# Seven products instead of eight in three groups of part 0, and attention issued in whole tiles

## The chip, the core and the metric

The kernel runs on one core of a Trainium2 chip. The metric is the time of one execution on the device in microseconds (us). The core has a matrix engine (TensorE; its products are called PE and its weight loads PEld below), VectorE (DVE), ScalarE (ACT), GpSimd (POOL) and a sequencer that issues the transfers (SP). They run side by side and wait for one another by semaphores. Products land in PSUM, which has 8 banks; DVE and ACT read them there, POOL cannot.

## The reference

Causal attention with a window of 128 positions and a slope per head, then two MLPs, all on 2304 tokens of 512 features, in float32:

```python
# attention: 4 sequences of 576 tokens, 8 heads of 64
scores = scale * q @ k.T
mask = (rel >= 0) & (rel < 128)            # rel = own position - other position
attn = softmax(where(mask, scores + bias, -1e9))
x = (attn @ v) as [2304, 512]
# first MLP, d_ff = 1536
g = x @ w_gate
x = (g * sigmoid(g) * (x @ w_val)) @ w_out
# second MLP, d_ff = 2048
h = x @ w_in
out = (h * sigmoid(h)) @ w_out2
```

The inputs arrive as 64-bit numbers.

## The kernel before

**Parts and groups.** The 18 tiles of 128 tokens are cut into three parts of 6 tiles, and a part into two halves of 384 tokens (N = 384). Each part goes through attention, the first MLP in G1 = 6 groups of 256 hidden features (`moe1`, for part 0 `moe1_plain`), and the second in G2 = 8 groups (`moe2`). The attention of part 1 runs between the MLP products of part 0, that of part 2 between those of part 1.

**Precision.** Each operand is held as a high and a low piece, and each product is three passes (hi·hi, hi·lo, lo·hi), lines 762 to 764, 906 to 908 and 936 to 938. So every value that becomes an operand is copied (mostly ACT, line 301) and the copy subtracted from it (POOL line 311 or DVE line 310).

**Plain groups and quads.** A plain group computes [256 features] x [512 inputs] x [two token halves] as eight block products, a quad as seven by Strassen's scheme (`quad`). A quad needs seven weight blocks: the three given ones A11, A12, A22 and four sums S1 to S4. It also needs seven activation blocks: `operands` makes them from the stored activations into the seven slots of `XOP` (slots 0, 1, 2 hold given blocks, 3 to 6 sums and differences). Part 0 uses plain groups in the first MLP: its attention writes the four given blocks straight into `XOP`, in slots 0, 1, 2 and 6.

**Weights.** `raw_weight` loads 64-bit weights and turns them into 32-bit words (ACT line 660, DVE line 663). In mode "raw" `quad_weights` makes the sums, splits all seven blocks and stores them to DRAM. In mode "kept" it loads the seven blocks. In mode "sum" (part 1, first MLP) it loads the stored words and three blocks, and makes and stores the four sums. All transfers are issued by SP from one queue in a written order.

**Order.** Every operation is entered into a `Plan` with its engine, a cost, a due time, what it reads and writes and the PSUM banks that it takes. `issue` then walks through a model of the engines and writes the instructions of each engine out in one fixed order. For a bank it keeps limits by kind: "mm" for MLP products, "S" for scores, "att" for all attention, and so on. So a change of costs, due times or dependencies moves instructions on every engine.

**Attention per half tile.** For each tile and each half of the heads: `prepare` turns k and q (PE lines 398 and 406, identity products), `score` makes 12 products on 64 rows of the array (line 448) into two banks, DVE masks and reduces, ACT takes exponents, POOL normalizes (line 497), PE turns the result (line 515), POOL cuts it into two triangles (lines 522 and 529), and `weigh` multiplies with v on 64 columns (line 541). The MLP products use the whole 128x128 array. `out1` and `out2` are the second products of the MLPs (lines 906 and 936); they lie in `pend` until `flush` enters them after the next group's first products, and DVE adds their results into `ACC` (lines 920 and 948).

Of the kernel before, what the change touches and what calls it, by code (L numbers as in the profile page):

```python
# [9 lines left out]
F32 = mybir.dt.float32  # L10
# [10 lines left out]
P = 128  # L21
# [180 lines left out]
def attention_moe_moe2_kernel(  # L202
# [32 lines left out]

    nc = tc.nc
# [9 lines left out]
    G1, G2 = F1 // (2 * P), F2 // (2 * P)  # L246
    NU, NO, NRAW, NW, NH, NTMP = 17, 3, 2, 3, 6, 8
# [33 lines left out]
    U_R = ring(2, [P, 4, P], F32, "u")  # L281
    L_R = ring(1, [P, 4, P], F32, "l")
# [11 lines left out]
    plan = Plan(BANKS, {"mm": 6, "att": 4, "T": 1, "S": 3, "C": 2, "O": 1, "B": 4})  # L294
# [129 lines left out]
    def attend(i, hf, dues):  # L424
        n = 2 * i + hf
        qt, qk = QT_R[n % len(QT_R)], ("qt", n % len(QT_R))
# [5 lines left out]
        heads = slice(4 * hf, 4 * hf + 4)  # L432

        banks = [Bank("S"), Bank("S")]

        def score():
            for p in range(2):
                for x, y in ((0, 0), (0, 1), (1, 0)):  # L440
                    for e in range(2):
                        rows = slice(64 * e, 64 * e + 64)
                        view = banks[e].tile.rearrange("p (a b c) -> p a b c", a=2, b=2)
                        rhs = KR[rows, y, 2 * hf + p]
                        dst = view[:, p]
                        if first(i):
                            rhs, dst = rhs[:, s], dst[:, 0]
                        nc.tensor.matmul(  # L448
                            dst, qt[rows, x, p, :], rhs, start=(x == 0 and y == 0), stop=(x == 1)
                        )  # L450

        reads = [qk, ("KR", s, hf)] + ([] if first(i) else [("KR", 1 - s, hf)])
        plan.add("pe", 6 * 118 + 60, dues[0], score, reads, banks, take=tuple(banks))
# [55 lines left out]
        cb, ob = Bank("C"), Bank("O")  # L509
        cps = lambda: cb.tile.rearrange("p (a b) -> p a b", b=P)  # L510
        ops = lambda: ob.tile[:, 0:2 * P].rearrange("p (a b) -> p a b", b=P)
# [22 lines left out]
        parts = [(i, u)] if first(i) else [(i - 1, u), (i, lo)]  # L534

        def weigh():
            for p in range(2):
                for a, (tl, m) in enumerate(parts):
                    for j in range(2):
                        l = 2 * p + j  # L540
                        nc.tensor.matmul(  # L541
                            ops()[64 * j:64 * j + 64, p, :],
                            VLD_R[tl % len(VLD_R)][:, 4 * hf + l, :],
                            m[:, l, :],
                            start=(a == 0),
                            stop=(a == len(parts) - 1),
                        )

        reads = [uk] + ([] if first(i) else [lk]) + [x for tl, _ in parts for x in loaded(tl, "v", hf)]
        plan.add("pe", 540 * len(parts) + 60, due, weigh, reads, [ob], take=ob)  # L550
        ti = i % PT
        xt = XST[:, ti, 2 * hf:2 * hf + 2, :]
        xk = [("xt", ti, 2 * hf + p) for p in range(2)]
        if i >= PT:
            copy_op(256, due, lambda: xt, ops, [ob], xk, give=ob)
        else:
# [3 lines left out]
            copy_op(256, due, lambda: xh, ops, [ob], keys)  # L560
            plan.add(
                "dve", cost("dve", 256), due,
                lambda: nc.vector.tensor_tensor(xl, ops(), xh.bitcast(F32), ALU.subtract), [ob], keys, give=ob,  # L563
# [16 lines left out]
    def split(dst_slot, kk, src, reads, due, bank=None):  # L580
# [4 lines left out]
        copy_op(N, due, lambda: hi_ap, src, reads, keys, psum=psum)  # L585
        sum_op(N, due, lambda: lo_ap, src, lambda: hi_ap.bitcast(F32), ALU.subtract, reads, keys, give=bank, psum=psum)

    def operands(src, name, due):

        due -= 25000.0  # L590

# [509 lines left out]
```

## Time and profile before

| | |
|---|---|
| median of 3 runs | 954.29 us (953.21 to 955.04) |
| the profiled execution | 954.24 us, of which the span from first to last instruction is 952.5 us |
| PE busy in the span | 931.7 us (98%) |
| DVE, ACT, POOL busy | 644.8, 499.2, 352.9 us (68%, 52%, 37%) |
| 16 DMA engines | 68.2% of their time, 219 GB/s of HBM traffic |
| mean granted TensorE clock | 0.998 of full speed |

Busy time of PE counts a product from its start to its modelled end, and products overlap in the array; so a stretch in which PE is busy throughout can still hold time that a different order of products would save. The distance from one product's start to the next one's start tells that. Parts 0, 1 and 2 of the MLPs take about 27 to 376, 376 to 660 and 660 to 952 us of the span.

### The profile page before, as it was taken

What the parts mean: (1) busy time and instruction counts of PE and PEld (TensorE: products, weight loads), DVE (VectorE), ACT (ScalarE), POOL (GpSimd) and SP (SyncE); (2) the same over time, 40 slices, a digit from 0 to 9 for tenths busy, and PEclk for the clock granted to TensorE, in tenths of its full rate; (3) what the DMA queues carried; (4) which work ended last, traced back from release to release, by engine and by line L of the source; (5) the groups of instructions that cost most, each with busy time, mean ns of one, the idle gap of its engine ahead of it and who ended that gap; (6) DMA issues with size and microseconds to landing.
All of it is one profiled execution on the core that took longest, in us unless ns stands there. A gap on an engine that the chain in (4) does not pass through costs nothing.

```text
span 952.5 us, 16827 instructions
## 1 busy us (share of the span) xinstructions
PE 931.7 (98%) x5662; PEld 854.8 (90%) x5662; DVE 644.8 (68%) x1489; ACT 499.2 (52%) x1269; POOL 352.9 (37%) x426
## 2 busy tenths in 40 slices
PE   7999999998999999999999999999999999999998
PEld 5888989998887888999999998888899999988886
DVE  7886666758798889557666756657745555855655
ACT  6877555556866765665453564345343323553331
POOL 2645333347666788796651521111200000300000
PEclk9999999999999999999999999999999999999999
DMA  9978897776578987998766666355466666654522
GB/s 216 276 240 253 271 301 260 256 241 207 189 255 262 293 266 259 362 285 287 227 200 185 198 201 191 125 167 184 162 239 201 208 214 215 204 198 170 161 89 89
DMA packets 156854, 209.78 MB, mean 220 GB/s; under 512 B 65760, under 2 KB 86496, under 8 KB 156768
## 3 DMA queue, kind: packets, MB, share of 16 engines
q1 hardware_dynamic: 156768, 208.71, 68.2%
q8 instruction: 45, 0.74, 0.3%
q14 instruction: 41, 0.34, 0.1%
HBM read 146.28 MB, written 62.39 MB: 219 GB/s over the span
## 4 chain that ended last, share of the span: by engine, by line
PE 86%; DVE 7%; DMA 3%; ACT 2%; POOL 1%; issue 1%; SPq 0%; DVEq 0%; ACTq 0%; POOLq 0%
PE bank L762 15%; PE bank L763 14%; PE bank L764 14%; PE bank L936 6%; PE bank L938 6%; PE bank L937 6%; PE bank L906 5%; PE bank L907 5%; PE bank L908 5%; PE bank L448 3%; PE bank L541 3%; DVE word L663 2%; PE bank L515 1%; DMA raw<-in_moe_w_in_dram 1%; DVE bank L464 1%
## 5 line engine op out<-in xcount | busy, mean ns | idle before, releaser
L762 PE MATMUL bank<-XOP,wu 128*128 128x384 f32 (+2 forms) x880 | 301.5, 343 | 6.7 <-DVE qt L412 2.1
L763 PE MATMUL bank<-XOP,wu 128*128 128x384 f32 (+2 forms) x880 | 293.8, 334 | 0.6 <-DVE XOP L563 0.5
L764 PE MATMUL bank<-XOP,wu 128*128 128x384 f32 (+2 forms) x880 | 294.0, 334 | 0.1
L762 PEld LDWEIGHTS bank<-XOP,wu 128*128 128x128 f32 x880 | 165.5, 188 | 15.9 <-ACT tmp L301 2.8
L763 PEld LDWEIGHTS bank<-XOP,wu 128*128 128x128 f32 x880 | 165.8, 188 | 2.2 <-DVE XOP L563 0.7
L764 PEld LDWEIGHTS bank<-XOP,wu 128*128 128x128 f32 x880 | 165.6, 188 | 0.4 <-POOL wu L311 0.4
L311 POOL TENSOR_TENSOR h<-tmp,h 128x384 fp32r<-128x384 f32 x67 | 71.3, 1074 | 194.7 <-ACT h L301 186.4
L301 ACT ACTIVATE tmp<-bank 128x384 f32<-128x384 f32 x140 | 65.5, 489 | 108.1 <-PE bank L764 73.3
L936 PE MATMUL bank<-wo,h 128*128 128x512 f32 x290 | 116.1, 400 | 0.5 <-DVE ACC L948 0.5
L938 PE MATMUL bank<-wo,h 128*128 128x512 f32 x290 | 114.0, 393 | 0.0
L937 PE MATMUL bank<-wo,h 128*128 128x512 f32 x290 | 113.9, 393 | 0.0
L948 DVE TENSOR_TENSOR ACC<-bank,ACC 128x512 f32<-128x512 f32 (+1 forms) x127 | 86.0, 682 | 32.5 <-PE bank L938 32.0
L865 DVE SCALAR_TENSOR_TENSOR tmp<-tmp,bank 128x384 f32<-128x384 f32 (+2 forms) x128 | 68.6, 544 | 53.4 <-ACT tmp L855 43.7
L906 PE MATMUL bank<-h,wo 128*128 128x384 f32 (+2 forms) x296 | 100.9, 341 | 0.0
L907 PE MATMUL bank<-h,wo 128*128 128x384 f32 (+2 forms) x296 | 98.5, 333 | 0.6 <-POOL h L311 0.6
L908 PE MATMUL bank<-h,wo 128*128 128x384 f32 (+2 forms) x296 | 98.6, 333 | 0.0
L802 DVE TENSOR_TENSOR bank<-bank,tmp 128x384 f32<-128x384 f32 x96 | 53.8, 561 | 52.9 <-PE bank L764 41.1
L301 ACT ACTIVATE h<-tmp 128x384 fp32r<-128x384 f32 x102 | 52.5, 521 | 61.3 <-PE bank L937 35.2
L920 DVE TENSOR_TENSOR ACC<-bank,ACC 128x384 f32<-128x384 f32 x120 | 65.3, 553 | 22.8 <-PE bank L908 22.5
L855 ACT ACTIVATE tmp<-bank 128x384 f32<-128x384 f32 (+2 forms) x134 | 63.2, 482 | 32.7 <-PE bank L764 19.4
L311 POOL TENSOR_TENSOR wu<-word,wu 128x256 fp32r<-128x256 f32 x69 | 52.3, 775 | 61.9 <-ACT wu L301 47.4
L497 POOL TENSOR_TENSOR c<-c,st 128x512 f32<-128x512 f32 x36 | 39.1, 1087 | 93.6 <-DVE st L494 91.1
(98 smaller groups left out, 1580.5 us busy)
## 6 DMA issues: line engine op xcount, KB each, us to landing
wo<-kept_o SPq DMA_DIRECT2D x56, 512.0 KB, 4.1
wu<-kept_i SPq DMA_DIRECT2D x112, 256.0 KB, 3.6
wu<-kept_g SPq DMA_DIRECT2D x60, 256.0 KB, 3.6
wu<-kept_v SPq DMA_DIRECT2D x60, 256.0 KB, 3.9
raw<-in_moe_w_out_dram SPq DMA_DIRECT2D x28, 512.0 KB, 4.6
kept_o<-wo SPq DMA_DIRECT2D x28, 512.0 KB, 3.8
kept_i<-wu SPq DMA_DIRECT2D x56, 256.0 KB, 2.9
kept_g<-wu SPq DMA_DIRECT2D x42, 256.0 KB, 4.3
```

The source lines that it names most:

```text
L301: act = lambda: nc.scalar.activation(out(), src(), AF.Copy)
L311: pool = lambda: nc.gpsimd.tensor_tensor(out(), x(), y(), op)
L762: nc.tensor.matmul(ps, wh, xh, start=start, stop=False, skip_group_check=True)
L763: nc.tensor.matmul(ps, wh, xl, start=False, stop=False, skip_group_check=True)
L764: nc.tensor.matmul(ps, wl, xh, start=False, stop=stop, skip_group_check=True)
L906: nc.tensor.matmul(ps[:, 0:n], wh, h[:, 0], start=(i == 0), stop=False)
L907: nc.tensor.matmul(ps[:, 0:n], wh, h[:, 1], start=False, stop=False)
L908: nc.tensor.matmul(ps[:, 0:n], wl, h[:, 0], start=False, stop=(i == 1))
L936: nc.tensor.matmul(ps, hh, wh, start=(i == 0), stop=False)
L937: nc.tensor.matmul(ps, hh, wl, start=False, stop=False)
L938: nc.tensor.matmul(ps, hl, wh, start=False, stop=(i == 1))
L948: plan.add("dve", cost("dve", n), due, lambda: nc.vector.tensor_tensor(acc, pv(), acc, ALU.add), [b], keys, give=b)
```

## The change

1. Part 0's first MLP uses plain groups only for groups 0 to 2 (GP = 3). `restore` puts part 0's attention output, high plus low piece, into `XST`; `operands` with `plain=False` makes the four slots 3 to 6 that are sums; and groups 3 to 5 run as quads in mode "raw". Part 1 then takes groups 3 to 5 in mode "kept".
2. From tile 6 on (EARLY = 6) the scores of both halves of a tile are one plan entry that takes four banks, and so are the two weighings, into one bank. The buffers `u` and `l` get one more each, the "S" limit goes from 3 to 4, "att" from 4 to 6. A copy of 512 columns takes the weighed tile to `XST`, instead of two of 256.
3. The out-products of the second token half are entered before those of the first, in `moe1` and `moe2`.
4. Part 1's attention gets due times 33 us apart, three tiles before the border between the two MLPs and three from 20 us behind it. Before, the six tiles were spread evenly.

```diff
+    EARLY = 6
+    GP = 3
...
-    U_R = ring(2, [P, 4, P], F32, "u")
-    L_R = ring(1, [P, 4, P], F32, "l")
+    U_R = ring(3, [P, 4, P], F32, "u")
+    L_R = ring(2, [P, 4, P], F32, "l")
...
-    plan = Plan(BANKS, {"mm": 6, "att": 4, "T": 1, "S": 3, "C": 2, "O": 1, "B": 4})
+    plan = Plan(BANKS, {"mm": 6, "att": 6, "T": 1, "S": 4, "C": 2, "O": 1, "B": 4})
...
+    def score(i, halves, due):
...
+        take = tuple(b for hf in halves for b in banks[hf])
+        plan.add("pe", 6 * 118 * len(halves) + 290, due, products, reads, list(take), take=take)
+        return banks
...
-        plan.add("pe", 6 * 118 + 60, dues[0], score, reads, banks, take=tuple(banks))
...
-        plan.add("pe", 540 * len(parts) + 60, due, weigh, reads, [ob], take=ob)
+        plan.add("pe", 218 * len(halves) * (1 if first(i) else 2) + 290, due, product, reads, [ob], take=ob)
...
+    def restore(due):
...
+        for j in range(2):
+            for blk in range(2):
+                for kk in range(2):
+                    c, slot = 2 * j + kk, x_slot(j, blk)
+                    hi, lo = (tiles(XOP[:, slot, i, kk].bitcast(F32)) for i in range(2))
+                    dst = XST[:, blk * BT:blk * BT + BT, c, :]
+                    sum_op(
+                        N, due, lambda dst=dst: dst, lambda hi=hi: hi, lambda lo=lo: lo, ALU.add,
+                        x_keys(slot, kk), [("xt", blk * BT + t, c) for t in range(BT)],
+                    )
...
-            for hf in range(2):
-                prepare(i, hf, at(i + 0.5 * hf) - 8000.0)
-                attend(i, hf, [at(i + p / NP) for p in (2 * hf, 2 * hf + 1)])
+            for halves in [(0,), (1,)] if i < EARLY else [(0, 1)]:
+                t0 = at(i + 0.5 * halves[0])
+                for hf in halves:
+                    prepare(i, hf, t0 - 8000.0)
+                banks = score(i, halves, t0)
+                for hf in halves:
+                    attend(i, hf, [at(i + p / NP) for p in (2 * hf, 2 * hf + 1)], banks[hf])
+                weigh(i, halves, at(i + 0.5 * halves[-1] + 1 / NP))
...
-            for b in range(2):
+            for b in (1, 0):
...
-            for t in range(PT):
+            for t in (*range(BT, PT), *range(BT)):
...
     attention_part(0, ramp)
     moe1_plain([0])
-    spread(1, state["t"] + 6000.0, M1 * (G1 - 1) / G1 + M2 - 8000.0)
-    moe1_plain(range(1, G1))
+    t_next = state["t"] + 6000.0
+    moe1_plain(range(1, GP))
+    restore(state["t"] - 10000.0)
+    operands(XST, "xt", state["t"], plain=False)
...
+    t_moe2 = t_next - 6000.0 + (G1 - GP) * 22 * pe_cost(6, N) + (GP - 1) * 24 * pe_cost(6, N)
+    early = lambda x: t_next + 0.0 + (x - PT) * 33000.0
+    attention_part(1, lambda x: early(x) if x < PT + PT // 2 else t_moe2 + 20000.0 + (x - PT - PT // 2) * 33000.0)
+    moe1(0, range(GP, G1), "raw", False)
     flush()
     operands(ACC, "acc", state["t"])
...
-    moe1(1, range(G1), "sum", False)
+    moe1(1, range(GP), "sum", False)
+    moe1(1, range(GP, G1), "kept", False)
```

Three places show what the plan makes of it. The first is PE at the end of part 1's second MLP, where the last attention tile of part 2 is weighed between out-products (`wo` and `h` are the out-product's operands, `u`, `l` and `vld` the weighing's). Before, the second half of the tile, with the first half 120 rows earlier:

```order
L938 MATMUL bank_138<-wo_92,h_103 128x512
L541 MATMUL bank_139<-u_131,vld_122 64x128 x2
L541 MATMUL bank_139<-l_132,vld_123 64x128 x2
L541 MATMUL bank_139<-u_131,vld_122 64x128 x2
L541 MATMUL bank_139<-l_132,vld_123 64x128 x2
L936 MATMUL bank_133<-wo_91,h_108 128x512
```

and in the changed kernel:

```order
L982 MATMUL bank_139<-wo_92,h_104 128x512
L563 MATMUL bank_138<-u_131,vld_122 64x128 x2
L563 MATMUL bank_138<-l_133,vld_123 64x128 x2
L563 MATMUL bank_138<-u_131,vld_122 64x128 x2
L563 MATMUL bank_138<-l_133,vld_123 64x128 x2
L563 MATMUL bank_138<-u_132,vld_122 64x128 x2
L563 MATMUL bank_138<-l_134,vld_123 64x128 x2
L563 MATMUL bank_138<-u_132,vld_122 64x128 x2
L563 MATMUL bank_138<-l_134,vld_123 64x128 x2
L980 MATMUL bank_142<-wo_91,h_107 128x512
```

Both halves now stand in one run of PE, in one bank; the score products are joined in the same way. Counted over all of PE's rows, runs of score products that follow a product of the full array (an MLP product or a turn) go from 34 to 22, runs of weighings from 34 to 20, and PE has 36 rows fewer, all of them of lines 762 to 764.

The second place is POOL while part 0's first MLP is in its later groups (`word` is a converted weight, `wu` a split block, `sum` one of S1 to S4). Before, in a stretch of the plain groups:

```order
L311 TENSOR_TENSOR wu_74<-word_97,wu_74 128x256
L522 AFFINE_SELECT l_132<-u_130 128x512
L529 AFFINE_SELECT u_130<-u_130 128x512
L311 TENSOR_TENSOR wo_91<-word_98,wo_91 128x512
L311 TENSOR_TENSOR wu_76<-word_98,wu_76 128x256
L311 TENSOR_TENSOR wu_75<-word_98,wu_75 128x256
L311 TENSOR_TENSOR wu_77<-word_96,wu_77 128x256
```

and in the changed kernel, for one quad of group 3:

```order
L314 TENSOR_TENSOR sum_99<-word_96 128x256
L314 TENSOR_TENSOR sum_100<-sum_99,word_98 128x256
L314 TENSOR_TENSOR sum_101<-word_98,word_96 128x256
L314 TENSOR_TENSOR sum_102<-word_98,sum_100 128x256
L314 TENSOR_TENSOR wu_88<-sum_100,wu_88 128x256
L314 TENSOR_TENSOR wu_89<-sum_99,wu_89 128x256
L314 TENSOR_TENSOR wu_73<-word_98,wu_73 128x256
L314 TENSOR_TENSOR wu_76<-word_96,wu_76 128x256
```

The four sums and their splits, which stood in part 1, now stand here. Between the first of the 24 sums of groups 3 to 5 and the first sum of the second MLP, POOL has 88 operations: 40 splits of weight blocks, 24 sums, 9 splits of hidden values, 10 selections, 4 normalizations and 1 split of an out-weight.

The third place is DVE at the border between part 0's two MLPs, where `operands` turns `ACC` into the slots of `XOP`. Before (`st`, `KR` and `qt` belong to attention, `word` to a weight):

```order
L605 TENSOR_TENSOR bank_137<-ACC 128x384
L605 TENSOR_TENSOR bank_136<-ACC,bank_137 128x384
L310 TENSOR_TENSOR XOP<-bank_140,XOP 128x384
L401 TENSOR_TENSOR KR<-bank_133,KR 128x2x128
L310 TENSOR_TENSOR XOP<-bank_136,XOP 128x384
L310 TENSOR_TENSOR XOP<-bank_137,XOP 128x384
L493 TENSOR_SCALAR st_128<-st_128 128x4
L494 RECIPROCAL st_128<-st_128 128x4
L663 SCALAR_TENSOR_TENSOR word_96<-raw_93,top_95 128x512
L605 TENSOR_TENSOR bank_137<-ACC 128x384
L802 TENSOR_TENSOR bank_135<-bank_135,tmp_111 128x384
L412 SCALAR_TENSOR_TENSOR qt_125<-bank_133,qt_125 128x256
```

and in the changed kernel:

```order
L415 SCALAR_TENSOR_TENSOR qt_124<-bank_137,qt_124 128x256
L649 TENSOR_TENSOR bank_140<-ACC 128x384
L649 TENSOR_TENSOR bank_139<-ACC,bank_140 128x384
L404 TENSOR_TENSOR KR<-bank_135,KR 128x2x128
L649 TENSOR_TENSOR bank_138<-ACC 128x384
L313 TENSOR_TENSOR XOP<-bank_139,XOP 128x384
L649 TENSOR_TENSOR bank_137<-ACC,bank_138 128x384
L313 TENSOR_TENSOR XOP<-bank_140,XOP 128x384
L415 SCALAR_TENSOR_TENSOR qt_125<-bank_141,qt_125 128x256
L313 TENSOR_TENSOR XOP<-bank_137,XOP 128x384
L313 TENSOR_TENSOR XOP<-bank_138,XOP 128x384
```

The preparation of an attention tile (`KR`, `qt`) still stands among the operands; the softmax (`st`) and the weight conversion (`word`) no longer do.

## Rows read from the trace of the kernel before

**Rows 1.** The page, part 1: busy us, share of the span, instructions.

```profile
PE 931.7 (98%) x5662; PEld 854.8 (90%) x5662; DVE 644.8 (68%) x1489; ACT 499.2 (52%) x1269; POOL 352.9 (37%) x426
```

**Rows 2.** Windows: length, busy PE, PEld, DVE, ACT, POOL, clock, DMA share, GB/s.

```profile
0.00:27.00 27.00, 20.45 (x151) 14.99 (x151) 21.30 (x102) 18.50 (x67) 7.77 (x15) 1.00 0.89 215
...
146.00:229.00 83.00, 83.00 (x539) 80.01 (x538) 56.37 (x133) 47.17 (x118) 39.31 (x50) 1.00 0.76 248
...
229.00:241.00 12.00, 9.44 (x47) 7.72 (x47) 11.40 (x24) 8.74 (x20) 6.17 (x5) 0.88 0.62 182
241.00:376.00 135.00, 131.15 (x740) 112.56 (x739) 111.96 (x213) 94.34 (x234) 102.27 (x118) 1.00 0.79 258
376.00:830.00 454.00, 452.66 (x2702) 425.70 (x2701) 285.90 (x641) 208.24 (x518) 143.09 (x172) 1.00 0.65 213
```

**Rows 3.** Timeline of PE, twelve full-array products of 384 columns: start, length.

```profile
303.94 0.33 PE L762 MATMUL bank<-XOP,wu 128*128 128x384 f32 x1
...
305.85 0.34 PE L764 MATMUL bank<-XOP,wu 128*128 128x384 f32 x1
```

**Rows 4.** Timeline of products and weight loads around one run of scores.

```profile
316.06 0.40 PE L938 MATMUL bank<-wo,h 128*128 128x512 f32 x1
...
316.38 0.75 PEld L448 LDWEIGHTS bank<-KR,qt 64*128 64x128 f32 x12 [0.36 <-issue]
...
317.26 0.19 PEld L762 LDWEIGHTS bank<-XOP,wu 128*128 128x128 f32 x1
317.27 0.45 PE L762 MATMUL bank<-XOP,wu 128*128 128x384 f32 x1
...
317.55 0.34 PE L763 MATMUL bank<-XOP,wu 128*128 128x384 f32 x1
```

**Rows 5.** Timeline of PE around one run of weighings.

```profile
434.60 0.34 PE L908 MATMUL bank<-h,wo 128*128 128x384 f32 x1
...
435.14 0.39 PE L541 MATMUL bank<-l,vld 128*64 128x128 f32 x4
...
435.57 0.39 PE L541 MATMUL bank<-l,vld 128*64 128x128 f32 x4
435.89 0.44 PE L906 MATMUL bank<-h,wo 128*128 128x384 f32 x1
436.17 0.34 PE L907 MATMUL bank<-h,wo 128*128 128x384 f32 x1
```

**Rows 6.** Timeline at the border of part 0's MLPs, on PE, DVE and POOL.

```profile
236.83 0.44 PE L762 MATMUL bank<-XOP,wu 128*128 128x384 f32 x1 [2.07 <-DVE qt L412]
...
233.99 0.68 DVE L663 SCALAR_TENSOR_TENSOR word<-raw,top 128x512 int32<-128x512 int32 x1
234.59 1.40 DVE L605 TENSOR_TENSOR bank<-ACC 128x384 f32<-128x384 f32 x1
...
234.16 1.41 POOL L497 TENSOR_TENSOR c<-c,st 128x512 f32<-128x512 f32 x1 [1.82 <-DVE st L494]
```

**Rows 7.** Windows of two later stretches, columns as in rows 2.

```profile
376.00:430.00 54.00, 53.18 (x322) 49.75 (x321) 32.65 (x78) 33.85 (x92) 42.83 (x56) 1.00 0.93 314
...
400.00:425.00 25.00, 24.39 (x157) 23.03 (x156) 12.13 (x29) 15.99 (x44) 23.62 (x31) 1.00 0.92 285
```

**Rows 8.** Groups by shape on DVE: count, busy us, mean ns, idle before.

```profile
L605 DVE TENSOR_TENSOR bank<-ACC,bank 128x384 f32<-128x384 f32 x12 | 6.6, 560 | 0.4
```

**Rows 9.** Windows, instructions of line 762 alone, then of line 906 alone.

```profile
146.00:229.00 83.00, 30.95 (x91) 16.94 (x91) 1.00 0.76 248
...
146.00:229.00 83.00, 16.94 (x48) 9.02 (x48) 1.00 0.76 248
```

**Rows 10.** The page, part 6: transfers, size of each, us to landing.

```profile
raw<-in_moe_w_out_dram SPq DMA_DIRECT2D x28, 512.0 KB, 4.6
...
kept_g<-wu SPq DMA_DIRECT2D x42, 256.0 KB, 4.3
```

More of the change, by code (lines that the diff above doesn't have):

```diff
@@ L422, in prepare, with products, attend @@
         plan.add("dve", cost("dve", 256), due, q_lo, [bq], [qk], give=bq)
-    def attend(i, hf, dues):
+    def score(i, halves, due):
+        s = i % 2
+        banks = {hf: (Bank("S"), Bank("S")) for hf in halves}
+        def products():
+            for hf in halves:
+                qt = QT_R[(2 * i + hf) % len(QT_R)]
+                for p in range(2):
+                    for x, y in ((0, 0), (0, 1), (1, 0)):
+                        for e in range(2):
+                            rows = slice(64 * e, 64 * e + 64)
+                            view = banks[hf][e].tile.rearrange("p (a b c) -> p a b c", a=2, b=2)
+                            rhs, dst = KR[rows, y, 2 * hf + p], view[:, p]
+                            if first(i):
+                                rhs, dst = rhs[:, s], dst[:, 0]
+                            nc.tensor.matmul(
+                                dst, qt[rows, x, p, :], rhs, start=(x == 0 and y == 0), stop=(x == 1)
+                            )
+        reads = [("qt", (2 * i + hf) % len(QT_R)) for hf in halves]
+        reads += [("KR", t, hf) for t in ((s,) if first(i) else (s, 1 - s)) for hf in halves]
+        take = tuple(b for hf in halves for b in banks[hf])
+        plan.add("pe", 6 * 118 * len(halves) + 290, due, products, reads, list(take), take=take)
+        return banks
+    def attend(i, hf, dues, banks):
         n = 2 * i + hf
-        qt, qk = QT_R[n % len(QT_R)], ("qt", n % len(QT_R))
         s = i % 2
@@ L431, in attend @@
         uk, lk = ("uu", us), ("l", ls)
[L432 to L452, printed above, removed]
-        plan.add("pe", 6 * 118 + 60, dues[0], score, reads, banks, take=tuple(banks))
         def scores(e, due):
@@ L611, in operands @@
         t1, t2 = {}, {}
-        for kk in range(2):
+        for kk in range(2 if plain else 0):
             split(0, kk, *b[0, 0, kk], due)
@@ L619, in operands @@
             split(4, kk, t1[kk][0], t1[kk][1] + t2[kk][1], due, bank=t1[kk][1][0])
-        for kk in range(2):
+        for kk in range(2 if plain else 0):
             split(1, kk, *b[1, 0, kk], due)
@@ L624, in operands @@
             split(6, kk, *t3, due, bank=t3[1][0])
-        for kk in range(2):
+        for kk in range(2 if plain else 0):
             split(2, kk, *b[1, 1, kk], due)
@@ L923, in out2 @@
         done = g == G2 - 1
-        last = done and part == 2 and t == PT - 1
+        last = done and part == 2 and t == BT - 1
         for c0, n in [(0, DM // 2), (DM // 2, DM // 2)] if last else [(0, DM)]:
@@ L1013, in moe1 @@
             flush()
-            ws = [out_weight("o1", 2 * g + i, False, t0 - WLEAD + 15000.0) for i in range(2)]
+            ws = [out_weight("o1", 2 * g + i, part == 0, t0 - WLEAD + 15000.0) for i in range(2)]
             cv, state["t"] = quad(vw, state["t"])
```

69 lines of the change are left out of this document (43 added, 26 removed).

## The prediction

> **What bounds the kernel now.** I read the busy shares first, then the windows, then single starts on PE. PE is busy 931.7 of 952.5 us, DVE 68%, ACT 52%, POOL 37% [rows 1]: the matrix engine's stream is the kernel, and 20.8 us in all are left in which it stands still. The windows say where: 6.6 us of them in the ramp of the first 27 us, 2.6 around the border of part 0's two MLPs, 3.9 in part 0's second MLP, only 1.3 in the 454 us behind it; the 83 us of the last plain groups have none [rows 2]. So idle time can give little. A change must shorten the stream itself or keep it from growing holes.
>
> Busy time hides something, though. Twelve full-array products of 384 columns start within 1.91 us, 11 steps of 0.1736 us [rows 3]; that is PE's real pace. Around a run of scores the pace breaks. From the start of the product before the run to the second product behind it 1.49 us pass [rows 4]. A 512-column product takes 0.1736 x 512/384 = 0.23 and the first product behind the run 0.17, which leaves 1.09 us for the run. Its own pace: twelve weight loads in pairs span 0.75 us, one load takes 0.19, so six pairs start (0.75 - 0.19)/5 = 0.11 us apart [rows 4], 0.67 us for six. The other **0.41 us is the price of going from the full array to 64-row products and back**. The run of weighings: 1.57 us from the product before it to the second behind it [rows 5], less two products of 0.17 is 1.22; eight products take 0.43 us, sixteen of them (four lines) 0.86; the price is **0.36 us**. PE counts as busy through all of that.
>
> **The change part by part.** The sum is made against the profiled execution: 954.24 us, 1.7 us more than its span, next to a median of 954.29.
>
> *Seven products for eight.* A plain group has 8 blocks x 2 matrices x 2 x 3 = 96 first products, a quad group 84; three groups save 36 products of 384 columns, as PE's rows count them. PE had no idle time there [rows 2]: 36 x 0.1736 = **-6.2 us**. This is the best known term.
>
> *Whole tiles.* 12 runs of scores and 14 of weighings fewer: 12 x 0.41 + 14 x 0.36 = **-9.9 us**. Nothing covers the break before, since PE is the engine all others wait for. The bound below: if each joined run has to wait for its second half or for its banks as long as the break that it saves, the term is 0; I take it whole, because the plan can put other products ahead of a run that isn't ready, and half of it (-5) for the range.
>
> *Where the sums go.* The 24 sums and their splits for groups 3 to 5 leave part 1, where PE waits for almost nothing (so that gives at most the 1.3 us of that window), and enter part 0. How long is that stretch? The 83 us window holds 3 x 91 first and 3 x 48 second products [rows 9], 417 of the three plain groups' 432; 83.0 + 15 x 0.17 - 6.2 = 79.4 us for the three quad groups with their attention. POOL did 118 operations in 102.3 us of the second MLP [rows 2], 0.87 each; the 88 operations of the new stretch are 76 us, 96% of it, against 39.3 of 83 before. What that costs is read where POOL was as full: in 25 us with 23.6 of POOL, PE lost 0.6 [rows 7], 2.4%; in the second MLP, with POOL at 76% and DVE at 83%, 3.9 of 135, 2.9% [rows 2]. 79.4 us at 2.4 to 2.9% is 1.9 to 2.3; I take **+2.3 us**, with 0 below and the GpSimd rival's price above. `restore` (8 additions) lies early, in groups 1 and 2, with POOL half empty. The first border, plain to quads, I put at nothing: of the four new slots only one (6) still has to wait for the plain products, its fifth place among the seven leaves 24 products (4.2 us) ahead of it, and the out-products of group 2 stand there too. Without that cover it would be the price of the old border, 2.6 us.
>
> *The old border.* Between 229 and 241 us PE stands 2.6 us, and the granted clock is 0.88, which loses another 12 x 0.12 = 1.4 us [rows 2]. The longest wait, 2.07 us, ends at 236.83 [rows 6]. It stands behind a DVE subtraction of two `ACC` blocks that takes 1.40 us at 234.59, while POOL normalizes scores from 234.16 to 235.57 [rows 6]; the same kind of operation with one operand in a bank takes 0.56 [rows 8]. So softmax and a weight conversion were in the way, and the changed order has neither between the operands. It still has two `KR` and two `qt`, and PE's second product needs a slot behind some eight DVE operations, so I keep 2.2 of the 4.0 us: **-1.8 us** (bounds -4 and +1). Second token half first helps here: the block that both first steps of `operands` need is done earlier.
>
> What this row shows has a rule. The Trainium skill, SBUF — State Buffer, section "SBUF: two separate sides", says that VectorE and GpSimd share a pair of ports as an exclusive lock: a DVE operation with two SBUF inputs blocks for the whole of a GpSimd operation. The trace agrees here, 1.40 against 0.56 us. The rule speaks against this change, since it fills POOL; by the row's 2.4% the stretch costs 2.3 us, by the rule taken strictly what the second rival gives.
>
> *The rest.* One more `u` and `l` buffer, the larger limits and the 33 us spacing move waits of which part 1 has 1.3 us in all. Copies of 512 columns instead of twice 256 are ACT's, at 52%. Fetches and stores balance: 24 transfers of words go, 24 of blocks come. Nothing is taken for these. The second MLP of part 0 keeps its kind of work and its 3.9 us.
>
> Sum: 954.2 - 6.2 - 9.9 + 2.3 - 1.8 = **938.6 us**.
>
> **The rivals.**
>
> *The banks take back the joining.* Scores of a whole tile need four of eight banks free at once, and each comes back only after DVE has masked and reduced it. If PE then lacks banks for MLP products, holes of about 0.4 us appear behind each joined run. For it: four banks are twice what was held before. Against: a quad needs three, an out-product one. Then the second term is gone: 938.6 + 9.9 = 948.5 us.
>
> *POOL and DVE become the bound of the new stretch.* If no DVE operation with both inputs in SBUF ran while POOL runs, 76 us of POOL and DVE's 18 weight conversions at 0.68 [rows 6] and some 6 two-buffer products at 0.56, 15.6 us, would have to follow one another: 92 us for 79.4, +12.6 in place of +2.3: 948.9 us. For it: the 1.40 us row. Against: the 25 us at 94% POOL that cost 0.6, and weights of the first quads can be made ahead, beside plain groups with POOL at half.
>
> *Transfers become the bound, and the kernel slower.* The stretch moves 18 raw weights and 6 stores of out-weights of 512 KB, 42 stores of 256 KB [rows 10] and q, k, v of two tiles (6 x 256 KB): 25.2 MB, 317 GB/s over 79.4 us. The stretch it replaces ran at 248 [rows 2]. At that rate it takes 101.6 us, 22.2 more: 954.2 - 6.2 - 9.9 - 1.8 + 22.2 = 958.5 us. It decides from 254 GB/s downward (99.1 us). Against: 54 us at 314 GB/s with a DMA share of 0.93 [rows 7], and 248 GB/s went with a share of 0.76 only, so the queue had room.
>
> *The change does not do what it says* is ruled out for the counts: PE's rows show 36 products and 26 runs fewer.
>
> *Better than the sum:* the 3.9 us of the second MLP and the rest of the border vanish as well: 938.6 - 3.9 - 2.2 = 932.5 us.
>
> **How the numbers follow.** The sum as worked out, with its own range of 934 to 944, gets 0.65. The banks get 0.11, POOL and DVE 0.14, transfers 0.05, better than the sum 0.05. The range of 933 to 949 us holds the first three cases and leaves out the transfers and part of the best case and of the worse tails. A measurement of this kernel can tell about 0.2% (1.9 us) from no change, so faster means under 952.4 and slower over 956.2. Everything but the transfers lies under 952.4: faster 0.94; the transfers at rates a little above 254 GB/s would be the same, 0.03; slower 0.03.
>
> **What would show it.** The 36 products by the counts of lines 806 to 808. The joining by PE's timeline: a run of 24 score products should take 0.41 us less than two runs of 12 did, and the product behind it should start without a wait; a wait on a bank there speaks for the first rival. The new stretch by its windows: PE idle near 2 us of 80, POOL over 85%; if PE lost 8 us or more with POOL or DVE named, it is the second rival, with a DMA share at 0.95 and raw weights named the third. The border: a wait of under 2 us in place of 2.07 and a clock near 1.00. The prediction is wrong if the stream of PE gets shorter by 16 us and the span doesn't.

## The result, and the profile after

The changed kernel takes 940.98 us (median of 4 runs, 939.86 to 942.73) beside 954.61 for the kernel before: a ratio of 0.9863, 95% interval [0.9846, 0.9880]. The forecast was 938.6 us with a main range of 934 to 944. In a later group of five rounds, beside three other kernels on one chip, the same kernel gave 943.46 us, ratio 0.9909 [0.9889, 0.9929]: the gain is 9 to 14 us, and the group in which it is measured matters by some 4. The profiled execution took 940.32 us, span 938.6, 13.9 less than before [rows 1].

The page of the changed kernel, part 1, which answers to [rows 1]: busy us, share, instructions.

```profile
PE 918.6 (98%) x5626; PEld 847.7 (90%) x5626; DVE 668.7 (71%) x1520; ACT 501.2 (53%) x1272; POOL 380.4 (41%) x436
```

36 rows of PE are gone, and PE is busy for 13.1 us less: the stream got shorter, the holes did not. Without the ramp, in windows from the first MLP product to the span's end, before and then after:

```profile
26.34:952.50 926.16, 911.62 (x5512) 839.96 (x5512) 624.14 (x1391) 481.32 (x1205) 345.21 (x412) 1.00 0.68 220
24.94:938.60 913.66, 899.47 (x5480) 834.09 (x5480) 647.93 (x1422) 483.36 (x1210) 371.79 (x421) 1.00 0.68 223
```

PE is busy for 12.1 us less there and idle for 14.2 us where it was 14.5. Windows of the changed kernel, which answer to [rows 2] (length, busy PE, PEld, DVE, ACT, POOL, clock, DMA share, GB/s):

```profile
134.00:217.00 83.00, 82.34 (x535) 80.13 (x534) 68.80 (x132) 56.28 (x138) 68.05 (x79) 1.00 0.84 279
217.00:231.00 14.00, 10.95 (x54) 9.15 (x53) 13.18 (x27) 10.74 (x28) 9.57 (x12) 0.94 0.50 154
231.00:363.00 132.00, 129.36 (x725) 112.44 (x723) 116.38 (x227) 93.51 (x234) 106.42 (x114) 0.99 0.84 277
363.00:817.00 454.00, 451.46 (x2734) 427.76 (x2734) 286.75 (x637) 202.28 (x494) 116.20 (x135) 1.00 0.63 207
```

The new quad stretch (first window) lets PE stand for 0.66 us of 83 with POOL at 82% and DVE at 83%. The border behind it costs 3.05 us of idle time where [rows 2] had 2.56, and in the 454 us behind part 0, which hold two more borders, PE stands 2.54 us where it stood 1.34.

By stages, each from its first product on PE's timeline to the next stage's (us; part 2 began at 684.1 before, later than the 660 given ahead):

| stage | begins, before | begins, after | change in length |
|---|---|---|---|
| ramp | 0 | 0 | -1.4 |
| part 0, groups 0 to 2 | 26.3 | 24.9 | +0.2 |
| part 0, groups 3 to 5 | 135.6 | 134.4 | -8.7 |
| part 0's second MLP and part 1's group 0 | 227.6 | 217.7 | -0.3 |
| the rest of part 1 | 396.8 | 386.6 | -3.5 |
| part 2 to the span's end | 684.1 | 670.4 | -0.2 |

Two joined runs, PE's timeline of the changed kernel, which answer to [rows 4, 5]:

```profile
382.02 0.34 PE L808 MATMUL bank<-XOP,wu 128*128 128x384 f32 x1
382.29 1.65 PE L449 MATMUL bank<-KR,qt 64*128 64x256 f32 x24
383.87 0.45 PE L806 MATMUL bank<-XOP,wu 128*128 128x384 f32 x1
384.15 0.34 PE L807 MATMUL bank<-XOP,wu 128*128 128x384 f32 x1
...
420.23 0.34 PE L952 MATMUL bank<-h,wo 128*128 128x384 f32 x1
420.50 0.44 PE L563 MATMUL bank<-u,vld 128*64 128x128 f32 x4
...
422.39 0.45 PE L950 MATMUL bank<-h,wo 128*128 128x384 f32 x1
422.68 0.34 PE L951 MATMUL bank<-h,wo 128*128 128x384 f32 x1
```

Read as the prediction read the single runs: 24 score products take 384.15 - 382.02 - 2 x 0.17 = 1.78 us where two runs of 12 took 2.18, so one joining saves 0.40. The joined weighings, eight lines of four products, take 422.68 - 420.23 - 2 x 0.17 = 2.10 where two runs of 16 took 2.44: 0.34. Behind both the next product starts without a wait.

The border of part 0's MLPs, timeline of the changed kernel on PE, DVE and POOL (in brackets the idle time before and what ended it), which answers to [rows 6]:

```profile
217.06 6.56 POOL L314 TENSOR_TENSOR XOP<-ACC,XOP 128x384 fp32r<-128x384 f32 x6
218.99 1.40 POOL L314 TENSOR_TENSOR XOP<-ACC,XOP 128x384 fp32r<-128x384 f32 x1
218.97 0.55 DVE L649 TENSOR_TENSOR bank<-ACC 128x384 f32<-128x384 f32 x1
219.08 0.45 PE L807 MATMUL bank<-XOP,wu 128*128 128x384 f32 x1 [0.92 <-POOL XOP L314]
220.35 1.43 DVE L649 TENSOR_TENSOR bank<-ACC 128x384 f32<-128x384 f32 x1
222.30 0.45 PE L807 MATMUL bank<-XOP,wu 128*128 128x384 f32 x1 [0.55 <-DVE XOP L313]
226.79 0.44 PE L806 MATMUL bank<-XOP,wu 128*128 128x384 f32 x1 [0.46 <-ACT tmp L304]
227.15 0.68 DVE L707 SCALAR_TENSOR_TENSOR word<-raw,top 128x512 int32<-128x512 int32 x1
227.75 0.55 DVE L846 TENSOR_TENSOR bank<-bank,tmp 128x384 f32<-128x384 f32 x1
228.33 0.56 DVE L305 COPY tmp<-bank 128x384 f32<-128x384 f32 x1
228.95 0.51 PE L806 MATMUL bank<-XOP,wu 128*128 128x384 f32 x1 [0.83 <-DVE tmp L305]
```

The single wait of 2.07 us is gone; four of 0.5 to 0.9 (and one of 0.3) stand in its place. The first two are for low pieces of operands. No softmax lies here any more, yet one of DVE's subtractions of two `ACC` blocks is as long as before, 1.43 us where the one ahead of it took 0.55: POOL's six low pieces of the operands themselves (1.09 us each on average) run beside them now. The 0.55 was no free pass: the piece that POOL began 0.02 us behind that subtraction (the second line, a part of the first) took 1.40 where the two ahead of it took 1.0 each. The last two waits are for copies that the running quad takes out of a bank: on ACT behind three operand copies, and on DVE behind the last operand, the weight conversion at 227.15 and the sum at 227.75. So a weight conversion still stands in the way, behind the operands and no longer among them.

The next two borders have new or longer waits, same view:

```profile
529.07 0.41 PE L806 MATMUL bank<-XOP,wu 128*128 128x384 f32 x1 [0.23 <-ACT XOP L304]
534.41 0.45 PE L807 MATMUL bank<-XOP,wu 128*128 128x384 f32 x1 [0.24 <-DVE XOP L313]
539.93 0.44 PE L806 MATMUL bank<-XOP,wu 128*128 128x384 f32 x1 [0.31 <-ACT tmp L304]
...
809.40 0.44 PE L807 MATMUL bank<-XOP,wu 128*128 128x384 f32 x1 [1.09 <-POOL XOP L314]
```

### The profile page after: what moved, and what is told of

Same layout as the page of the kernel before. It is cut to its first block, busy times and chain, and to the rows that moved or that the text cites. A ratio compares the mean times of both kernels' runs of the same rounds, so it can differ in the third digit from the quotient of the medians.

```text
span 938.6 us, 16796 instructions
## 1 busy us (share of the span) xinstructions
PE 918.6 (98%) x5626; PEld 847.7 (90%) x5626; DVE 668.7 (71%) x1520; ACT 501.2 (53%) x1272; POOL 380.4 (41%) x436
## 4 chain that ended last, share of the span: by engine, by line
PE 63%; DVE 9%; DMA 5%; POOL 3%; ACT 3%; issue 2%; SPq 0%; DVEq 0%; ACTq 0%; POOLq 0%
PE bank L806 11%; PE bank L807 11%; PE bank L808 11%; PE bank L980 6%; PE bank L982 6%; PE bank L981 6%; PE bank L950 3%; PE bank L951 3%; PE bank L952 3%; PE bank L563 2%; DVE word L707 1%; POOL wu L314 1%; DVE bank L649 1%; DMA raw<-in_moe_w_out_dram 1%; DMA raw<-in_moe_w_in_dram 1%
## 5 line engine op out<-in xcount | busy, mean ns | idle before, releaser
L806 PE MATMUL bank<-XOP,wu 128*128 128x384 f32 (+2 forms) x868 | 296.6, 342 | 5.2 <-DVE tmp L305 2.3
L807 PE MATMUL bank<-XOP,wu 128*128 128x384 f32 (+2 forms) x868 | 290.5, 335 | 3.3 <-POOL XOP L314 2.0
L808 PE MATMUL bank<-XOP,wu 128*128 128x384 f32 (+2 forms) x868 | 290.0, 334 | 0.0
L806 PEld LDWEIGHTS bank<-XOP,wu 128*128 128x128 f32 x868 | 163.5, 188 | 13.4 <-ACT tmp L304 4.4
L807 PEld LDWEIGHTS bank<-XOP,wu 128*128 128x128 f32 x868 | 163.7, 189 | 6.1 <-POOL XOP L314 2.6
L314 POOL TENSOR_TENSOR h<-tmp,h 128x384 fp32r<-128x384 f32 x76 | 83.9, 1118 | 200.1 <-ACT h L304 197.8
L808 PEld LDWEIGHTS bank<-XOP,wu 128*128 128x128 f32 x868 | 163.6, 188 | 0.1
L304 ACT ACTIVATE tmp<-bank 128x384 f32<-128x384 f32 x157 | 73.0, 489 | 113.5 <-PE bank L808 72.3
L909 DVE SCALAR_TENSOR_TENSOR tmp<-tmp,bank 128x384 f32<-128x384 f32 (+2 forms) x134 | 71.3, 544 | 47.5 <-ACT tmp L899 34.0
L992 DVE TENSOR_TENSOR ACC<-bank,ACC 128x512 f32<-128x512 f32 (+1 forms) x127 | 85.5, 681 | 27.3 <-PE bank L982 26.9
L846 DVE TENSOR_TENSOR bank<-bank,tmp 128x384 f32<-128x384 f32 x108 | 60.5, 561 | 57.7 <-PE bank L808 43.2
L304 ACT ACTIVATE h<-tmp 128x384 fp32r<-128x384 f32 x113 | 58.0, 520 | 78.3 <-PE bank L981 45.6
L707 DVE SCALAR_TENSOR_TENSOR word<-raw,top 128x512 int32<-128x512 int32 x68 | 63.4, 932 | 10.5 <-ACT top L704 6.5
```

The source lines that it names most:

```text
L304: act = lambda: nc.scalar.activation(out(), src(), AF.Copy)
L314: pool = lambda: nc.gpsimd.tensor_tensor(out(), x(), y(), op)
L806: nc.tensor.matmul(ps, wh, xh, start=start, stop=False, skip_group_check=True)
L807: nc.tensor.matmul(ps, wh, xl, start=False, stop=False, skip_group_check=True)
L808: nc.tensor.matmul(ps, wl, xh, start=False, stop=stop, skip_group_check=True)
L992: plan.add("dve", cost("dve", n), due, lambda: nc.vector.tensor_tensor(acc, pv(), acc, ALU.add), [b], keys, give=b)
```

## The experiments

The theory is the prediction's: the gain is 36 products and 26 breaks of the array's tiling, and the rest of the change costs or gives little. Its rivals are that banks take back the joining, or that POOL and DVE are the end of the quad stretch. Twelve runs followed in three groups, each group on one chip beside the kernel before. As the changed kernel itself stood at 0.9863 first and at 0.9909 in the last group, differences across groups are sure to some 4 us only, and a loss is given against both. "Behind the ramp" is the profiled span from the first MLP product on. It is split into the time in which PE stands idle, what PE lost to the lower clock (the profile has the clock at full or at half; a stretch of 3.4 us at half loses 1.7), and the rest, which is PE's stream itself. A span is one execution's: that of two_plain lies 3.5 us above its median time, that of all_plain 2.1 above, that of same_again 2.3 below. So a difference of spans under some 3 us shows nothing by itself; the stream does better, 897.8 and 898.0 us in two executions of the changed kernel.

| kernel | median us | ratio to before | span | first product | behind the ramp | idle | low clock | stream |
|---|---|---|---|---|---|---|---|---|
| before | - | 1 | 952.5 | 26.3 | 926.2 | 14.6 | 1.7 | 909.9 |
| changed | 940.98 | 0.9863 | 938.6 | 24.9 | 913.7 | 14.2 | 1.7 | 897.8 |
| weigh_halves | 945.27 | 0.9922 [0.9900, 0.9944] | 943.3 | 27.3 | 916.1 | 14.7 | 0 | 901.4 |
| all_plain | 946.96 | 0.9935 [0.9913, 0.9958] | 947.0 | 25.2 | 921.8 | 17.8 | 1.7 | 902.3 |
| first_half_first | 944.85 | 0.9900 [0.9866, 0.9934] | 944.4 | 27.1 | 917.2 | 17.2 | 0 | 900.0 |
| slot0_dve | 947.77 | 0.9952 [0.9925, 0.9980] | 947.7 | 25.2 | 922.5 | 21.2 | 3.4 | 897.9 |
| halves_mm5 | 954.03 | 1.0009 [0.9984, 1.0033] | 953.3 | 26.1 | 927.2 | 18.6 | 3.4 | 905.2 |
| whole_mm5 | 952.07 | 0.9979 [0.9958, 1.0000] | 950.3 | 27.1 | 923.2 | 21.6 | 1.7 | 899.9 |
| even_spread | 947.38 | 0.9929 [0.9905, 0.9954] | 945.3 | 27.2 | 918.1 | 16.7 | 3.4 | 898.0 |
| two_plain | 946.77 | 0.9942 [0.9921, 0.9963] | 948.6 | 28.9 | 919.7 | 17.7 | 5.1 | 896.9 |
| same_again | 943.46 | 0.9909 [0.9889, 0.9929] | 939.5 | 25.4 | 914.0 | 16.1 | 0 | 898.0 |
| shift_1us | 944.47 | 0.9918 [0.9899, 0.9937] | 943.1 | 28.2 | 914.9 | 16.8 | 0 | 898.1 |
| shift_10us | 946.82 | 0.9944 [0.9926, 0.9962] | 945.7 | 25.5 | 920.2 | 19.6 | 1.7 | 898.8 |
| first_half_again | 943.32 | 0.9909 [0.9889, 0.9929] | 941.6 | 25.1 | 916.5 | 15.8 | 1.7 | 899.0 |

**Weighings in halves again** (weigh_halves).

```diff
-                weigh(i, halves, at(i + 0.5 * halves[-1] + 1 / NP))
+                for hf in halves:
+                    weigh(i, (hf,), at(i + 0.5 * hf + 1 / NP))
```

> The changed kernel with the weighing of each half tile entered by itself again, the scores still joined: 13 runs of weighings more on PE (33 in place of 20). If the stream of PE is the time and each run costs its break: 13 x 0.36 = +4.7 us over the changed kernel's 941.0, so 945.7. If the gain came from waits that the other edits removed: no difference, 941.

0.9922 is 1.2 to 5.6 us over the changed kernel by its two ratios, and 2.4 us behind the ramp. The expected 4.7 lies inside; the trace shows 13 more runs. PE's stream is 3.6 us longer, 0.28 a run where the row's price is 0.36. The joining of weighings is worth three quarters of its price on PE; how much of that reaches the time is not settled closer than 1.2 to 5.6.

**All six groups of part 0 plain** (all_plain).

```diff
-    GP = 3
+    GP = 6
...
-    restore(state["t"] - 10000.0)
-    operands(XST, "xt", state["t"], plain=False)
```

> All six groups of part 0's first MLP plain again, the sums back in part 1; whole tiles, order and spacing as changed. If 36 products are worth what they take in PE's stream: +6.2 us less the 0.7 us that PE now idles in the quad groups, +5 to +6.2, 946 to 947. If the fuller POOL and DVE eat much of it there or at the border behind: +3 or less, 944 or under.

2.5 to 6.9 us by the ratios, 8.1 behind the ramp. Of the 8.1, 3.6 are more idle time, most of it in part 0's second MLP (8.2 us of idle time in the window from 231 to 363 where the changed kernel has 2.6). The stream is 4.5 longer, with two breaks fewer (0.8), where the 36 products are priced 6.2: most of their price is there.

**Scores and weighings in halves or whole, with one MLP bank fewer** (halves_mm5, whole_mm5). Both have five MLP banks, since the new limits on attention's banks leave no order for halves throughout beside six. The second edit below is that of halves_mm5 alone.

```diff
-    plan = Plan(BANKS, {"mm": 6, "att": 6, "T": 1, "S": 4, "C": 2, "O": 1, "B": 4})
+    plan = Plan(BANKS, {"mm": 5, "att": 6, "T": 1, "S": 4, "C": 2, "O": 1, "B": 4})
...
-    EARLY = 6
+    EARLY = 18
```

> The changed kernel with half tiles throughout (EARLY = 18) and the limit of banks for MLP products at 5 in place of 6; compare with whole_mm5, which has that limit alone. 12 runs of scores and 10 of weighings more on PE than whole_mm5. If each costs its break: 12 x 0.41 + 10 x 0.36 = 8.5 us more than whole_mm5. If joining pays by something else, or its banks take the gain back: under 3 us more.

> The changed kernel with the limit of banks for MLP products at 5 in place of 6. Control for halves_mm5. Within 2 us of 941 if banks are not short; some us more if they are.

The difference is 0.0030 of the ratio, 2.9 us, and 4.0 behind the ramp, not 8.5: the stream of the whole tiles is 5.3 shorter, their idle time 3.0 longer. By stages: from part 1's second group to part 2 the halves took 684.8 - 398.6 = 286.2 us, the whole tiles 682.0 - 400.4 = 281.6, the full price of that part's 12 breaks (4.6). In part 0 the whole tiles gained nothing (373.3 us against 372.5 from the first product on). Waits of PE from 25 to 400 us in whole_mm5 (us in total, times, longest):

```profile
PE bank L806 <- ACT tmp L304: 6.0, 7, 2.0
PE bank L563 <- DVE qt L415: 2.6, 1, 2.6
PE bank L806 <- DVE tmp L861: 2.1, 3, 1.3
```

First products wait for `tmp`, the copies and sums that a quad takes out of a bank before the next product goes into it. The changed kernel's waits of this kind from 217 to 363 us, where all of them in part 0 lie:

```profile
PE bank L806 <- DVE tmp L305: 2.3, 2, 1.4
PE bank L806 <- ACT tmp L304: 1.4, 2, 0.9
```

That is 8.1 us of such waits with five banks and 3.7 with six. So where banks are short the first rival is real; that the missing bank is what leaves these copies uncovered is argued, not shown. And one bank costs about as much as the whole joining was to bring: whole_mm5 is 7 to 11 us over the changed kernel.

**Two plain groups, not three** (two_plain): `GP = 2`.

> As changed, with four groups as quads in place of three (GP = 2), so 12 products fewer. If the stretch still has room on POOL and DVE: -12 x 0.1736 = -2.1 us, 938.9. If POOL and DVE (the second rival) are at their end: no gain or a loss, 941 to 945.

It lost 3 to 7.5 us by the ratios, 6.0 behind the ramp, where 12 fewer products should have given 2.1. Its windows, columns as above:

```profile
25.00:134.00 109.00, 106.31 (x850) 98.08 (x851) 92.14 (x274) 80.11 (x237) 76.30 (x93) 0.97 0.85 264
134.00:217.00 83.00, 80.17 (x511) 75.82 (x510) 72.08 (x141) 53.64 (x135) 65.82 (x73) 1.00 0.86 281
```

PE stands 2.83 us in the 83, 0.66 in the changed kernel, and 2.7 in the 109 with DVE at 85%, 1.75 in the changed kernel; there `tmp` and `XOP` are named. The stream is 0.9 us shorter; 3.5 more idle time and 3.4 more of low clock outweigh it in this execution, the slowest of ten. So a fourth quad group does not pay; that POOL and DVE are then at their end, as the second rival has it, is likely from these waits, but the low clock has as large a part.

**The old, even spacing of part 1's attention** (even_spread).

```diff
-    attention_part(1, lambda x: early(x) if x < PT + PT // 2 else t_moe2 + 20000.0 + (x - PT - PT // 2) * 33000.0)
+    spread(1, t_next, M1 * (G1 - 1) / G1 + M2 - 8000.0)
```

> The changed kernel with part 1's attention spread evenly again over both MLPs. If spacing keeps the border free: the softmax and its conversions come back among the operands, the border's idle time goes from 3 us to 4 or more and the clock falls: +1 to +2, 942 to 943. If the border is bound by its own chain either way: 941 within 0.7.

It lost 2 to 6.3 us by the ratios, 4.4 behind the ramp, of which 2.5 is idle time and 1.7 low clock; the stream is the same. Its waits from 217 to 240 us begin with

```profile
PE bank L409 <- DVE KR L404: 2.9, 1, 2.9
```

A q transpose waits for a `KR` piece that DVE makes late. What DVE did before it:

```profile
232.03 0.70 DVE L707 SCALAR_TENSOR_TENSOR word<-raw,top 128x512 int32<-128x512 int32 x1
232.65 0.55 DVE L649 TENSOR_TENSOR bank<-ACC 128x384 f32<-128x384 f32 x1
233.12 0.96 DVE L476 COPY_PREDICATED bank<-m_up,bigt 128x256 f32<-128x256 uint8 x1
234.54 0.42 DVE L404 TENSOR_TENSOR KR<-bank,KR 128x256 fp32r<-128x256 f32 x1
```

A weight conversion and the masking of scores stand among the operands again (L476, and the reducing behind it), and with them a wait of the old 2.07 us's kind. This is what the spacing keeps away.

**The first slot's low pieces on DVE** (slot0_dve).

```diff
+        if dst_slot == 0 and not psum:
+            plan.add(
+                "dve", cost("dve", N), due,
+                lambda: nc.vector.tensor_tensor(lo_ap, src(), hi_ap.bitcast(F32), ALU.subtract), reads, keys, port=True,
+            )
+            return
```

> As changed, but the low piece of slot 0 is always subtracted on DVE (0.55 us) and never on POOL (1.0 us). If the waits of the first product at the borders are that subtraction: 0.5 us less at each of the borders of parts 0 and 2, -1 to -1.5, 939.5 to 940. If the border is bound by DVE's whole chain, which gets two operations longer: no difference or up to +1.

It lost 4 to 8.5 us by the ratios where a gain of 1 to 1.5 or at most a loss of 1 was expected. The wait for POOL at the border went, but PE waits 1.42 and 0.49 us for the same pieces from DVE (at 219.23 and 220.51 us), and DVE got later for all behind it: 7.0 us more idle time (waits of PE, 217 to 363 us; its lines stand 6 lower):

```profile
PE bank L812 <- DVE tmp L867: 5.2, 2, 3.0
PE bank L812 <- ACT tmp L304: 3.3, 4, 1.6
```

**The order of the token halves** (first_half_first, first_half_again: one kernel, twice).

```diff
-            for b in (1, 0):
+            for b in (0, 1):
```

> The out-products of the first MLP in the old order, first token half first; all else as changed. In the trace of the changed kernel the first product of the second MLP waits 0.9 us in part 0 and 1.1 us in part 2 for the low piece of slot 0, which is made from the first token half, now the last to be finished. If that is what the new order costs: these two waits go and the time falls by 1 to 2.5 us, to 938.5 to 940. If the prediction's step is right and the new order helps the border: +1 to +3, 942 to 944.

> The first token half's out-products first, again, now beside the changed kernel on one chip. By the prediction's step, that the second half first brings the operands' first blocks earlier: 2.5 to 4 us slower than the changed kernel (its first run gave 0.990 to 0.9863, 3.5 us, with intervals that touch). If the order of the halves is worth nothing: within 1 us.

The first run looked like a loss of 3.5 us. Beside the changed kernel on one chip it was 943.32 to 943.46: nothing, within the some 2.7 us that two such intervals leave. The traces have it 2.5 and 3.2 us longer behind the ramp than same_again, the times do not. Half of the first reading was the ramp: its first product came at 27.1 us, the second time at 25.1, with the same code.

**The yardstick, and attention due 1 and 10 us later** (same_again, shift_1us, shift_10us): `t_moe2 + 21000.0` and `t_moe2 + 30000.0` for `t_moe2 + 20000.0`.

> The changed kernel itself, as a yardstick on the same chip for the three beside it. All theories: a ratio of 0.986 to the kernel before, within 0.984 to 0.988, and a span near 938.6 us.

> The second batch of part 1's attention is due 1 us later (21 for 20 us behind the border); the work, its counts and its lines stay. Theory A, the experiments' losses of 4 to 6 us come from what each undoes: a shift of 1 us does nothing, within 1 us of the changed kernel. Theory B, the order behind the edit is dealt anew by any small move, and some of those losses are only that: 2 to 6 us slower, with waits of other names at part 0's border and in its second MLP.

> The same batch due 10 us later (30 for 20 us behind the border), so that the preparation of its q and its softmax leave the border for the second MLP. If they are what holds the border's operands up: PE's idle time at the border falls from 3.05 to under 2 us and the low clock behind it (1.7 us) shrinks with it, 1.5 to 2.5 us faster than the changed kernel. If the sums and subtractions of the operands themselves hold it up (POOL's six sums of 1.09 us, DVE's subtraction of 1.43): the border keeps 3 us and the time stays within 1 us. If any move of the order costs: 2 to 6 us slower.

The yardstick missed its own expectation of 0.984 to 0.988, though its span agreed. 1 us later is 1.0 us slower by the medians, within the interval: theory A, as far as one small move can tell; the order of the halves, which costs nothing, says the same. Its span is 3.6 longer, but 2.8 of that is the ramp. Windows of the ramp in same_again, then in shift_1us:

```profile
0.00:25.00 25.00, 19.59 (x145) 14.35 (x146) 20.01 (x97) 17.60 (x61) 8.64 (x15) 1.00 0.95 232
```

```profile
0.00:25.00 25.00, 19.59 (x116) 13.91 (x116) 18.50 (x86) 16.16 (x55) 8.54 (x15) 0.90 0.94 228
```

As much busy time, 29 products fewer: PE ran part of it at the lower clock. 10 us later is 3.4 us slower, and does not test what it was made for. First its window of the border, then two of DVE's rows in it:

```profile
217.00:231.00 14.00, 11.14 (x58) 9.20 (x57) 13.83 (x29) 10.69 (x27) 9.55 (x11) 1.00 0.52 160
```

```profile
219.36 0.41 DVE L415 SCALAR_TENSOR_TENSOR qt<-bank,qt 128x256 fp32r<-128x256 f32 x1
220.81 0.42 DVE L404 TENSOR_TENSOR KR<-bank,KR 128x256 fp32r<-128x256 f32 x1
```

The border keeps its waits (2.86 us of idle time), but it also keeps its two `qt` (the second at 223.82 us) and its `KR`: the due time moved and they did not. So whether they hold the border up is untested. The loss lies at the border to part 1. Its longest wait, which ends at 384.11 us:

```profile
PE bank L806 <- DVE XOP L313: 4.1, 1, 4.1
```

The copy of part 1's last attention tile to `XST`, here and then in the changed kernel:

```profile
377.91 0.57 ACT L304 ACTIVATE XST<-bank 128x512 f32<-128x512 f32 x1
```

```profile
365.13 0.60 ACT L304 ACTIVATE XST<-bank 128x512 f32<-128x512 f32 x1 [2.47 <-PE bank L563]
```

Part 1's operands are made from `XST`, and the tile came 12.8 us later.

No experiment beat the changed kernel.

## Why the prediction held, and which step failed

*Seven products for eight, -6.2.* Held: 36 rows fewer, and all_plain, which has them back, has most of the price back on PE's stream.

*Whole tiles, -9.9.* Held in size per run, 0.40 and 0.34 us for 0.41 and 0.36, with 26 runs fewer, 9.6 us. But not all of it is left on PE's stream: the experiments that undo joinings find 0.28 us a run (weigh_halves) and 0.24 (halves_mm5 against whole_mm5). Part 1 pays the full price even at five banks; in part 0 five banks give it back in waits, and with six no run tells part 0 apart. The first rival is right at five banks; at six the runs don't show it.

*POOL and DVE in the quad stretch, +2.3.* Too high: PE stands 0.66 us there, by the window that was 83.00 of 83 before. That POOL works longer shows on DVE: the weight conversions (L663 before, L707 now) last longer, by a group on the page of the changed kernel

```profile
L707 DVE SCALAR_TENSOR_TENSOR word<-raw,top 128x512 int32<-128x512 int32 x68 | 63.4, 932 | 10.5 <-ACT top L704 6.5
```

932 ns on average against 833 before, 68 of them in both kernels. PE's waits in the stretch name none of them (its one wait there, 0.5 us, is for POOL's piece of a hidden value). So the port rule that the prediction weighed (the Trainium skill, SBUF — State Buffer, section "SBUF: two separate sides") is seen again in the 1.43 us subtraction beside POOL's pieces; where another came first and took 0.55, it was POOL's piece that took 1.40. Taken strictly over the whole stretch (the second rival) it would have cost 12.6 us, and the window refutes that. The transfers ran at 279 GB/s, above the 254 from which the third rival would have decided.

*The old border, -1.8.* This step failed. It said that softmax and a weight conversion were in the way and that the changed order has neither between the operands. Softmax did leave, and the 2.07 us wait with it; even_spread, which brings both back, brings such a wait back. But other things are late next: POOL's pieces of 1.09 us each with DVE's subtraction beside them (waits of 0.92 and 0.55), and the quad's own copies, queued behind the operands on ACT and behind the operands and a weight conversion on DVE (0.46 and 0.83). Border and second MLP together, from the windows: before 2.56 + 3.85 us of idle time and 1.7 of low clock, 8.1 in all; now 3.05 + 2.64 idle and 1.7 of low clock, 7.4. The term measured **-0.7**. (The prediction took 1.4 for the low clock from its window of 12 us; the stretch at half clock ran on behind that window.) The second execution of the same kernel shows that the chain behind PE sets this, not the clock; its windows:

```profile
217.00:231.00 14.00, 11.07 (x59) 9.29 (x59) 13.83 (x29) 10.76 (x27) 9.56 (x11) 1.00 0.51 155
231.00:363.00 132.00, 127.36 (x719) 110.84 (x718) 115.95 (x226) 93.76 (x235) 105.73 (x114) 1.00 0.83 275
```

With the clock at 1.00 PE waits 2.93 + 4.64 = 7.6 us, a term of -0.5. Two of these waits come behind the stretch in which the first execution ran slow (229 to 233 us), and the first execution lacks them; same_again's PE timeline:

```profile
237.83 0.44 PE L806 MATMUL bank<-XOP,wu 128*128 128x384 f32 x1 [0.71 <-ACT tmp L304]
240.46 0.50 PE L980 MATMUL bank<-wo,h 128*128 128x512 f32 x1 [0.55 <-DVE st L483]
```

*"Second token half first helps here."* Fell: the order of the halves is worth nothing that the times can tell.

*The rest, nothing.* Not nothing, and the largest miss. The spacing is worth some 4 us against the even one in the changed kernel (even_spread; 2 to 6.3 by the ratios). By stages PE waits 1.0 us less in part 0's first three groups, 0.6 more in part 1 and 0.2 more in part 2, where the border's wait of 1.09 us, POOL's too, stands for one of 0.51. And the stream, for which nothing else was taken, holds 4.0 us more than the two terms above say.

The sum said -15.7; the profiled times differ by 13.9, of which 1.4 is the ramp, for which the sum had no term and which varies by more than that between executions of one kernel. Without the ramp it is 12.5: 0.4 from the waits and 12.1 from the stream, where products and whole tiles were to give 16.1. Counted from the starts of all of PE's products, the 36 products gave 6.2 and the runs of scores and weighings, with the products right behind them, 10.2, as priced. Against that, the identity products that turn k, q and the softmax, with the products right behind them, take 3.2 more than before (0.5 of it are four that lay in the ramp before), and short delays that count as busy some 1.2: PE counts as busy for about 0.17 us past the next product's due start, so a wait shorter than that shows nowhere as idle time. Why the identity products take longer is open.

So the forecast is closer than its terms. The stream was taken 4.0 us too short and the border 1.1 too good; the quad stretch was priced 1.6 too dear and the ramp gave 1.4 unasked, and those two made up for half of it by luck. What the two groups of runs, 0.4% apart, differ by is not explained either.

## What to carry to other kernels

A saving on the engine that all wait for can be priced from a few rows: the gap around a run of small products, less the products, gave 0.41 and 0.36 us and the joined runs gave back 0.40 and 0.34. That price holds for the run and not for the stream around it: of 16.1 us so priced 12.1 were left. A hole cannot be priced by taking its first cause away: list what the consumer needs and what stands in front of that on its engine, and see which is late next (here POOL's pieces, and a copy behind a weight conversion, in the same place). Compare spans from behind the ramp, split into idle time, low clock and stream, with the kernel itself in the group: the first reading of the token halves, 3.5 us, was a group and a ramp. And look whether an edit moved what it was to move, as shift_10us did not.

## What the runs showed of the hardware

The first 25 us ran at a granted clock of 1.00 in some executions and 0.90 to 0.93 in others, the two runs of one program with the first token half first among them (0.93 and 1.00). At 1.00 the first MLP product came at 24.9 to 26.3 us, at less at 27.1 to 28.9. In the changed kernel the clock fell behind the border, in one of two executions with nearly the same waits; windows of the one in which it fell:

```profile
229.00:231.00 2.00, 2.00 (x7) 2.00 (x8) 1.35 (x3) 1.91 (x6) 2.00 (x4) 0.55 0.64 244
231.00:233.00 2.00, 2.00 (x9) 2.00 (x8) 1.91 (x4) 1.55 (x4) 2.00 (x3) 0.60 0.26 98
```

The means lose 2 x 0.45 + 2 x 0.40 = 1.7 us, which is 3.4 of these 4 us at 1.2 GHz, the lower level, after 12 us in which PE had stood four times for 0.5 to 0.9 us and once for 0.3; and it cost the end nothing that the two traces can tell. Going from the full array to row-tiled products and back costs 0.41 us of PE around 12 products and 0.44 around 24 (1.78 us less 12 pairs at 0.11), and to column-tiled ones 0.36 around 16 and 0.38 around 32 (2.10 less eight lines at 0.215). A DVE subtraction of two SBUF operands, 0.55 us alone, took 1.43 when a POOL subtraction on SBUF began with it, and such a POOL subtraction, 1.0 alone, took 1.40 when DVE's had begun just before it.
